# Attention and a squared-relu feed-forward on one core: down-stage blocks formed from consecutive 128-token tiles

## The chip, the cores and the metric

The kernel runs on one core of a Trainium2 chip. The metric is the device time of an execution in microseconds (us); the time before is the median of three runs. The engines are TensorE (PE; its weight loads are PEld), VectorE (DVE), ScalarE (ACT), GpSimd (POOL) and SyncE (SP, which here issues stores and transposing DMAs). Each engine runs its own instruction stream in order; semaphores tie them together.

## The reference

```
scores = 1/sqrt(64) * q @ k.T            # 8 batches, 16 query heads on 4 kv heads, 384 tokens, 64 wide
x      = softmax(scores) @ v             # put back as 3072 tokens x 1024
h      = max(x @ w_in, 0)                # w_in 1024 x 2048
out    = (h * h) @ w_out                 # w_out 2048 x 1024, out 3072 x 1024 float32
```

## The kernel before

**Stages.** A batch is 384 tokens, three tiles of 128. Attention works in 64 units p, eight per batch (two heads each): scores in two halves of three PSUM banks, an exponential on ACT over each half (L482), attention products into the bank `po` (L495), a reciprocal and a multiplication on DVE (L503, L505), and a transposing DMA into xT. The feed-forward of a batch has an up stage of 16 tiles (128 of the 2048 hidden columns by 384 tokens; eight chunks of contraction, L536): the tile is evicted by DVE with the relu into `hr` (L542) and squared by ACT into h2T (L550). In the last batch POOL squares the odd tiles (L547). The down stage multiplies h2T by w_out.

**Two down stages.** Batches 0 and 1 use plain products (row_down, L585). From batch 2 on the work is done in blocks with seven products instead of eight, in Strassen's manner: a block takes one 128-token tile of each of two batches as two row halves, halves of the 2048 hidden columns, and halves of the 1024 output columns. Sums of weights are formed once (w_sums). The sums of the left side are formed by DVE for each block (a_sums: sums 1, 2 and 4 go into the buffer a_late, sum 3 overwrites h2T). down_pair handles tile i of batch 2m with tile i of batch 2m+1, for i = 0, 1, 2, after the up stages of both. The products go in the order 1, 6, 7, 2, 5, 4, 3; the last, 3, of the last block of a pair is put off (`carry`) to behind the next up tile, and at the very end it is done in two parts of 384 and 128 columns (L675), each added and stored by itself.

**Two row halves.** Each matmul uses 64 of the array's 128 rows; the lower half (lo) and the upper half (hi) of one contraction are separate instructions that overlap. `push` writes out all lo pieces of a job (an up tile is 8 pieces of 162.5 ns, a product 8 pieces of 216 ns), and puts its hi pieces into the queue `behind`; they follow 450 ns or more later by a clock that the program keeps while it writes the instructions. What follows a job (eviction, square, sums) is put in when its last hi piece is out, through the list `late` where it is delayed. A job takes one of four PSUM banks and frees it after its hi pieces. The program's clock decides order only; on the chip semaphores decide.

**Handing out.** The main loop over n (unit n from 8 to 64) writes score half 0, fill(0.4), the attention products of unit n-1, score half 1, fill(0.6). `fill(share)` adds the share to a credit and takes items from the feed-forward generator as long as the credit is above zero; an item costs its ns divided by PACE for its kind (up or down) and batch. An item is a whole up tile, a chunk of a plain product group, or a whole product. A batch's up stage may start when its last transposed x is taken to have landed (`usable`); until then the generator gives nothing and the credit is set to 0.

**Order of batches.** Up 0, down 0, up 1, down 1, up 2, up 3, three blocks, up 4, up 5, three blocks, up 6, up 7, three blocks. Two tiles of the even batch's up stage are held back (HELD) and come behind the odd batch's sixteen, which run in the order c, c + 8. The first block's sums are formed in two halves, at once after the square of the tile that completes them (`half`, `then`).

Of the kernel before, what the change touches and what calls it, by code (L numbers as in the profile page):

```python
# [106 lines left out]
def bass_gqa_attention__then__ffn_squared_relu_kernel(  # L107
# [326 lines left out]
    def push(lo, hi, done=None, prev=None, frees=()):  # L434
        while prev is not None and not prev["over"]:
            clock["lo"] += 100.0
            catch_up(clock["lo"])
        after = [prev["last"]] if prev is not None else ()
        total = 0.0
        for ns, fn in lo:  # L440
            catch_up(clock["lo"])
            last = fn(after)
            after = ()
            clock["lo"] += ns
            total += ns
        job = dict(hi=list(hi), ready=clock["lo"] + GAP, after=[last], done=done, over=False, frees=frees)
        behind.append(job)
        return job, total
# [40 lines left out]
    def row_attend(p, then=None):  # L489
# [27 lines left out]
        last_av[0] = push(lo, hi, done, last_av[0])[0]  # L517
# [4 lines left out]
    last_up = [None]  # L522

# [5 lines left out]
    def row_up(b, c, r, then=None):  # L529
# [11 lines left out]
        def done():  # L541
            R.add("vector", lambda e: e.tensor_scalar_max(hr[r][:, :], acc[:, 0:S], 0.0),  # L542
                  reads=[key], writes=[("hr", r)])

            def square():
                if b == B - 1 and c % 2:
                    R.add("gpsimd", lambda e: e.tensor_tensor(h2T[b % 2][:, c, :], hr[r][:, :], hr[r][:, :], ALU.mult),  # L547
                          reads=[("hr", r)], writes=h2(b, c))
                else:
                    R.add("scalar", lambda e: e.activation(h2T[b % 2][:, c, :], hr[r][:, :], AF.Square),  # L550
                          reads=[("hr", r)], writes=h2(b, c))
                if then:
                    then()

            late.append((clock["hi"] + 750.0, square))

        lo, hi = ([piece(h, kc) for kc in range(NKC)] for h in range(2))
        job, total = push(lo, hi, done, frees=(i,))
        last_up[0] = job
        return "up", total  # L560
# [7 lines left out]
    def store(y, b, i, jj, c0=0, c1=512):  # L568
        rows = out[b * S:(b + 1) * S, :].rearrange("(p j) f -> j p f", j=NJ)[i]
        R.add("sync", lambda e: e.dma_start(rows[:, jj * 512 + c0:jj * 512 + c1], y_sb[y][:, c0:c1]),  # L570
              reads=[("y", y)], writes=[("out", b, i, jj, c0)], dma=f"y{y}_{c0}")

    def row_down(b, jj):
        banks, jobs = [None] * NJ, [None] * NJ
        chunks = ((0, 6), (6, 11), (11, 16))
        for c0, c1 in chunks:
            for i in range(NJ):
# [20 lines left out]
                jobs[i], total = push(lo, hi, done if end else None, jobs[i], (banks[i],) if end else ())  # L598
                yield "down", total
# [27 lines left out]
    def a_sums(i, slots, which, c0=0, c1=NHC):  # L627
        t = slice(i * 128, i * 128 + 128)
        s1, s2, s4 = slots
        cs, ds = slice(c0, c1), slice(NHC + c0, NHC + c1)  # L630
        A11, A12, A21, A22 = (h2T[x][:, y, t] for x in range(2) for y in (cs, ds))
        k11, k12, k21, k22 = ([("h2T", x, y + c, i) for c in range(c0, c1)] for x in range(2) for y in (0, NHC))
        k1, k2, k4 = ([("a_sum", x, c) for c in range(c0, c1)] for x in slots)
        if 1 in which:
            tensor_op(a_sum[s1][:, cs], A21, A22, ALU.add, k21 + k22, k1 + EARLY_A)
# [7 lines left out]
    def product(n, m, i, slots, bank, first, done, prev=None, frees=()):  # L643
        s1, s2, s4 = slots
        t = slice(i * 128, i * 128 + 128)
        left = {1: (h2T[0], 0, 0, t), 2: (h2T[0], NHC, 0, t), 4: (h2T[1], NHC, 1, t), 7: (h2T[1], 0, 1, t),
                3: (a_sum[s4], 0, s4, None), 5: (a_sum[s1], 0, s1, None), 6: (a_sum[s2], 0, s2, None)}[n]
# [3 lines left out]
        def operands_of(c):  # L651
            a, c0, x, tt = left
            lk = ("a_sum", x, c) if tt is None else ("h2T", x, c0 + c, i)
            rk = {1: ("w_out", 0), 2: ("w_out", 0), 3: ("w_out", 1)}.get(n, ("wt", {4: 4, 5: 1, 6: 2, 7: 3}.get(n), c // 2))
            return a[:, c0 + c, :] if tt is None else a[:, c0 + c, tt], lk, rk

        def piece(h, c):
            rows = ROWS[h]
            lhs, lk, rk = operands_of(c)
            return 216.0, lambda after: R.add(  # L660
                "tensor", lambda pe: pe.matmul(acc, lhs[rows], right[rows, c], start=(first and h == 0 and c == 0),  # L661
                                               stop=(h == 1 and c == NHC - 1), skip_group_check=True),
                reads=[lk, rk], writes=[key], after=after)

        if callable(done):
            lo, hi = ([piece(h, c) for c in range(NHC)] for h in range(2))
            return push(lo, hi, lambda: done(acc, key), prev, frees)
# [13 lines left out]
        return None, 1.0  # L681

    def down_pair(m, slots):

        b0, b1 = 2 * m, 2 * m + 1
        final = b1 == B - 1
# [4 lines left out]
        def p1(q):  # L691
# [6 lines left out]
            q["p1"], t = product(1, m, q["i"], (0, 0, 0), q["e"], True, done)  # L698
            return "down", t

        def rest(q):
            i = q["i"]
            sl = q["slots"] = slots[i]
            alone = final and i == NJ - 1

            def run(n, bank, first, done, prev=None, frees=()):
                job, t = product(n, m, i, sl, bank, first, done, prev, frees)
                return job, ("down", t)

            bank = next_bank()  # L710
            yield run(6, bank, True, lambda acc, key: add(q["u"], q["u"], acc, key), frees=(bank,))[1]
            bank = next_bank()
            q["v"] = next_y()
            yield run(7, bank, True, lambda acc, key: add(q["v"], q["u"], acc, key), frees=(bank,))[1]

            def c11(acc, key):
                y = next_y()
                R.add("scalar", lambda e: e.copy(y_sb[y][:, :], acc), reads=[key], writes=[("y", y)])
                store(y, b0, i, 0)
                if i + 1 < NJ:  # L720
                    slots[i + 1] = take_sums()
                    a_sums(i + 1, slots[i + 1], (1, 2, 3))

            yield run(2, q["e"], False, c11, q["p1"], (q["e"],))[1]
            q["g"] = next_bank()

            def c22(acc, key):
                y = next_y()
                add(y, q["v"], acc, key)
                store(y, b1, i, 1)  # L730
                if i + 1 < NJ:
                    a_sums(i + 1, slots[i + 1], (4,))
                if alone:
                    add(q["u"], q["u"], acc, key)

            q["p5"], t = run(5, q["g"], True, c22, frees=(q["g"],) if alone else ())
            yield t

            def c21(acc, key):
                y = q["v"]  # L740
                tensor_op(y_sb[y][:, :], y_sb[y][:, :], acc, ALU.subtract, [key, ("y", y)], [("y", y)])
                store(y, b1, i, 0)

            bank = next_bank()
            yield run(4, bank, True, c21, frees=(bank,))[1]

        def p3(q):
            i = q["i"]

            def c12(acc, key):  # L750
                add(q["u"], q["u"], acc, key)
                store(q["u"], b0, i, 1)

            if final and i == NJ - 1:
                def part(f0, f1):
                    def fn(acc, key):
                        u = q["u"]
                        tensor_op(y_sb[u][:, f0:f1], acc[:, f0:f1], y_sb[u][:, f0:f1], ALU.add, [key, ("y", u)], [("y", u)])
                        store(u, b0, i, 1, f0, f1)
                    return f0, f1, fn  # L760

                return "down", product(3, m, i, q["slots"], None, True, [part(0, 384), part(384, 512)])[1]
            return "down", product(3, m, i, q["slots"], q["g"], False, c12, q["p5"], (q["g"],))[1]

        q = dict(i=0)
        yield p1(q)
        until(last_up[0])
        settle()
        upped.update((b0, b1))
        for i in range(NJ):  # L770
            yield from rest(q)
            if i + 1 < NJ:
                after = dict(i=i + 1)
                yield p1(after)
                yield p3(q)
                q = after
        carry.append(lambda: p3(q))

    HELD = 2
    tiles = [0]  # L780
    by_rows = [False]
    carry = []
    w_todo = [(n, part) for part in range(4) for n in (3, 2, 4)] + [(1, part) for part in range(4)]
# [20 lines left out]
    def feed_forward(b):  # L804
# [6 lines left out]
        order = [(b, c) for c in range(first, NFC)]  # L811
        if paired:
            order = [(b, c) for g in range(NHC) for c in (g, g + NHC)] + [(b - 1, c) for c in range(NFC - HELD, NFC)] \
                if b % 2 else order[:-HELD]
        slots = {}

        def half(x, which):
            if 0 not in slots:
                slots[0] = take_sums()
            a_sums(0, slots[0], which, x * NHC // 2, (x + 1) * NHC // 2)  # L820

        then = {}
        if paired and b % 2:
            then = {NHC - 1: lambda: half(0, (1, 2, 3, 4)), NFC - 1: lambda: half(1, (1, 2, 3)), len(order) - 1: lambda: half(1, (4,))}
        for n, (bb, c) in enumerate(order):
            if by_rows[0]:
                yield row_up(bb, c, tiles[0] % NHR, then.get(n))
            else:
                for k in range(0, NKC, 4):
                    yield up_step(bb, c, k, k + 4, tiles[0] % 2, tiles[0] % NHR)  # L830
            tiles[0] += 1
            if carry:
                yield carry.pop()()
# [4 lines left out]
        if paired and b % 2:  # L838
            yield from down_pair(b // 2, slots)
        elif not paired:  # L840
            last = last_up[0]
            for jj in range(2):
                for kind in row_down(b, jj):
                    yield kind
                    if last and last["over"]:
                        upped.add(b)


    def all_feed_forward():
        for b in range(B):  # L850
            while usable.get(b, float("inf")) > clock["lo"]:
                if carry:
                    yield carry.pop()()
                yield None
            yield from feed_forward(b)
        while carry:
            yield carry.pop()()
# [3 lines left out]
    PACE = {1: (3200.0, 3200.0), 2: (3700.0, 3100.0), 3: (3700.0, 3100.0), **{b: (5800.0, 3800.0) for b in range(4, B + 1)}}  # L861
# [124 lines left out]
```

The softmax here doesn't subtract the row's maximum and nothing guards it: scores larger than these inputs give would overflow.

## Time and profile before

| | us |
|---|---|
| median of three runs | 425.43 (425.27 to 425.53) |
| profiled execution, its own time | 424.85 |
| its span, first to last instruction | 422.8 |
| ACT exponential, one (L482, 112 of them) | 1.131 |
| ACT square, one (L550, 114) | 0.519 |
| POOL square, one (L547, 8) | 0.827 |
| DVE relu eviction, one (L542, 122) | 0.557 |
| DVE addition of a product to y, one (L603) | 0.69 |
| store of a y tile, issue to landing (L570, 47) | 2.0 |

Times in windows and timelines count from the first instruction. A window's row gives, for each engine, busy us and the number of instructions in brackets, in the order PE, PEld, DVE, ACT, POOL, then the granted clock (1.00 is full), the DMA share and GB/s. In the list of waits the numbers are us in total, times, and the longest in us. In a timeline a row is start, duration, engine, line, operation, out<-in, and in square brackets the idle time before it and what ended it. A matmul's end in these records is modelled, so two matmuls that follow each other overlap in them.

### The profile page before, as it was taken

The page shows a single profiled execution, that of the slowest core. Times are in us where ns is not written, and L with a number is a line of the kernel's source. Part 1 is how long each engine was busy: PE and PEld are TensorE (multiplying, and loading weights), DVE is VectorE, ACT ScalarE, POOL GpSimd, SP SyncE. Part 2 cuts the span into 40 slices and gives each one's busy share as a digit, 9 for nine tenths or more (in the row PEclk, how much of TensorE's full clock was granted, in tenths as well). Part 3 has the DMA queues.
Part 4 walks back from the last instruction along what each step waited for, and adds up shares of the span by engine and source line. Part 5 has one row for each costly group of instructions (what it writes and reads, how often), then busy time and mean ns, then how long its engine had stood idle before and what let it go on. Part 6 is the DMA issues. An engine that isn't in the chain of part 4 may idle for free.

```text
span 422.8 us, 13245 instructions
## 1 busy us (share of the span) xinstructions
PE 409.2 (97%) x6061; PEld 311.7 (74%) x6061; DVE 202.5 (48%) x419; ACT 213.0 (50%) x276; POOL 55.1 (13%) x70
## 2 busy tenths in 40 slices
PE   7999999999999999999999999999999999999995
PEld 4666877678767777877767788887676788858883
DVE  2664424278332555464563354555554354455442
ACT  4855764367755566665544556666554423112100
POOL 5831001021003000300021001200000000320000
PEclk9999999999999999999999999999999999999998
DMA  8999999639729931971229910980213220000222
GB/s 229 197 197 202 206 191 165 152 75 131 130 62 120 201 82 22 118 121 27 96 76 198 220 44 14 128 128 20 95 47 120 70 71 2 2 2 24 76 101 99
DMA packets 96103, 45.02 MB, mean 106 GB/s; under 512 B 74416, under 2 KB 90032, under 8 KB 96048
## 3 DMA queue, kind: packets, MB, share of 16 engines
q0 software_dynamic: 34288, 16.65, 31.6%
q1 hardware_dynamic: 58720, 25.28, 27.4%
q10 hardware_dynamic: 3040, 2.26, 1.8%
q8 instruction: 47, 0.77, 0.8%
q14 instruction: 8, 0.07, 0.0%
HBM read 35.65 MB, written 12.58 MB: 114 GB/s over the span
## 4 chain that ended last, share of the span: by engine, by line
PE 89%; ACT 4%; DVE 4%; DMA 2%; issue 1%; ACTq 0%; POOL 0%; DVEq 0%
PE sc_ps L536 16%; PE f_ps L536 16%; PE sc_ps L661 12%; PE f_ps L661 12%; PE po L495 12%; PE sc_ps L478 8%; PE f_ps L585 5%; ACT expT L482 3%; PE sc_ps L585 3%; PE f_ps L791 2%; DMA w_late<-in_q_dram 1%; DVE o_sb L505 1%; PE po L378 1%; PE sc_ps L361 1%; PE sc_ps L300 1%
## 5 line engine op out<-in xcount | busy, mean ns | idle before, releaser
L482 ACT ACTIVATE expT<-sc_ps 128x1152 bf16<-128x1152 f32 x112 | 126.7, 1131 | 102.1 <-PE sc_ps L478 64.1
L536 PE MATMUL sc_ps<-xT,w_in_sb 64*128 64x384 bf16 x992 | 146.6, 322 | 0.7 <-DVE hr L542 0.7
L536 PE MATMUL f_ps<-xT,w_in_sb 64*128 64x384 bf16 x960 | 142.2, 323 | 0.0
L536 PEld LDWEIGHTS sc_ps<-xT,w_in_sb 64*128 64x128 f16 x992 | 83.4, 94 | 15.3 <-DVE hr L542 1.1
L536 PEld LDWEIGHTS f_ps<-xT,w_in_sb 64*128 64x128 f16 x960 | 80.9, 94 | 13.2
L495 PEld LDWEIGHTS po<-v_aug,expT 64*128 64x128 bf16 x2016 | 76.1, 94 | 18.3 <-DVE o_sb L505 9.6
L550 ACT ACTIVATE h2T<-hr 128x384 bf16<-128x384 f32 x114 | 58.3, 519 | 52.6 <-DVE hr L542 52.6
L495 PE MATMUL po<-v_aug,expT 64*128 64x65 bf16 x2016 | 81.6, 190 | 2.3 <-DVE o_sb L505 2.1
L478 PE MATMUL sc_ps<-qT,kT 64*128 64x384 bf16 x336 | 57.1, 323 | 3.3 <-ACT expT L482 2.6
L542 DVE TENSOR_SCALAR hr<-f_ps 128x384 f32<-128x384 f32 x60 | 33.4, 557 | 38.9 <-PE f_ps L536 24.3
L542 DVE TENSOR_SCALAR hr<-sc_ps 128x384 f32<-128x384 f32 x62 | 34.3, 556 | 36.0 <-PE sc_ps L536 20.0
L661 PE MATMUL sc_ps<-w_out_sb,a_late 64*128 64x512 f16 x176 | 42.1, 376 | 0.0
L585 PE MATMUL sc_ps<-w_out_sb,h2T 64*128 64x512 f16 x192 | 41.5, 376 | 0.0
L585 PE MATMUL f_ps<-w_out_sb,h2T 64*128 64x512 f16 x192 | 39.7, 376 | 0.0
L661 PE MATMUL f_ps<-w_out_sb,h2T 64*128 64x512 f16 x160 | 38.7, 376 | 0.0
L661 PE MATMUL f_ps<-w_late,h2T 64*128 64x512 f16 x160 | 38.5, 376 | 0.0
L503 DVE RECIPROCAL rinv<-po 128x6 f32<-128x6 f32 x56 | 10.9, 195 | 47.5 <-PE sc_ps L585 16.8
L478 PEld LDWEIGHTS sc_ps<-qT,kT 64*128 64x128 bf16 x336 | 23.5, 94 | 13.6 <-ACT expT L482 9.9
L505 DVE TENSOR_TENSOR o_sb<-po,rinv 128x384 bf16<-128x384 f32 x56 | 31.2, 557 | 2.1 <-DVE rinv L503 0.2
L661 PE MATMUL sc_ps<-w_late,h2T 64*128 64x512 f16 x128 | 31.2, 376 | 0.0
L661 PE MATMUL sc_ps<-w_out_sb,h2T 64*128 64x512 f16 x128 | 30.9, 376 | 0.0
L603 DVE TENSOR_TENSOR y_sb<-sc_ps,y_sb 128x512 f32<-128x512 f32 x20 | 13.7, 691 | 26.3 <-PE sc_ps L661 15.0
(102 smaller groups left out, 426.4 us busy)
## 6 DMA issues: line engine op xcount, KB each, us to landing
out_dram<-y_sb SPq DMA_DIRECT2D x47, 256.0 KB, 2.0
q_next<-in_q_dram POOLq DMA_DIRECT2D x7, 768.0 KB, 10.6
w_in_sb<-in_moe_w_in_dram POOLq DMA_DIRECT2D x8, 512.0 KB, 12.4
w_out_sb<-in_moe_w_out_dram POOLq DMA_DIRECT2D x2, 2048.0 KB, 33.3
k_st<-in_k_dram POOLq DMA_DIRECT2D x7, 192.0 KB, 4.2
v_st<-in_v_dram POOLq DMA_DIRECT2D x7, 192.0 KB, 11.5
xT<-o_sb SPq DMA_TRANSPOSE x56, 3.0
w_late<-in_q_dram ACTq DMA_DIRECT2D x1, 768.0 KB, 8.6
```

Source lines behind the costliest of these rows:

```text
L478: "tensor", lambda pe: pe.matmul(sc_ps[:, i, 0:S], kt[rows, j * 128:(j + 1) * 128], qt[rows, :]),
L482: R.add("scalar", lambda e: e.activation(expT[p % NEX][:, 3 * half:3 * half + 3, :], sc_ps[:, 0:3, 0:S], AF.Exp, scale=0.125), reads=[("sc ...
L495: "tensor", lambda pe: pe.matmul(po_v[:, f % NJ, f // NJ, :], expT[p % NEX][rows, 2 * j + f % 2, f // 2 * 128:f // 2 * 128 + 128], v_aug[b ...
L503: R.add("vector", lambda e: e.reciprocal(rinv_v, po_v[:, :, :, D:D + 1]), reads=["po"], writes=[("rinv", p % 2)])
L505: R.add("vector", lambda e: e.tensor_tensor(o_sb[p % NO][:, :, :, :], po_v[:, :, :, 0:D], rinv_v.to_broadcast([128, NJ, 2, D]), ALU.mult), ...
L536: "tensor", lambda pe: pe.matmul(acc[:, 0:S], w_in_sb[rows, kc, c * 128:(c + 1) * 128], xT[b % NXT][rows, kc, :], start=(h == 0 and kc == ...
L542: R.add("vector", lambda e: e.tensor_scalar_max(hr[r][:, :], acc[:, 0:S], 0.0), reads=[key], writes=[("hr", r)])
L550: R.add("scalar", lambda e: e.activation(h2T[b % 2][:, c, :], hr[r][:, :], AF.Square), reads=[("hr", r)], writes=h2(b, c))
L585: "tensor", lambda pe: pe.matmul(acc, h2T[b % 2][rows, c, i * 128:(i + 1) * 128], w_out_sb[rows, c, jj * 512:(jj + 1) * 512], start=(h == ...
L603: R.add("vector", lambda e: e.tensor_tensor(out_ap, a, b, op), reads=reads, writes=writes)
L661: "tensor", lambda pe: pe.matmul(acc, lhs[rows], right[rows, c], start=(first and h == 0 and c == 0), stop=(h == 1 and c == NHC - 1), skip ...
L791: m = pe.matmul(acc[:, 0:S], w_in_sb[:, kc, c * 128:(c + 1) * 128], xT[b % NXT][:, kc, :], start=(kc == 0), stop=(kc == NKC - 1))
```

## The change

Blocks are formed from consecutive 128-token tiles: the tiles of batch 2, 3, 4 ... are put in a row, and after each up stage as many pairs as are complete are done: one block after batches 2, 4 and 6, two after 3, 5 and 7. The order becomes up 2, one block, up 3, two blocks, up 4, one block, and so on. A left-over tile (the third of an even batch) is paired with the first of the next batch. No tiles are held back; every batch from 2 on runs its up tiles in the order c, c + 8. The first block's sums are formed in three pieces (chunks 0-3, 4-6, 7), each written out 1.5 us, by the program's clock, after the square that completes it. All squares of up tiles are on ACT. `squared` records which squares have been written out; a product whose left side is read straight from h2T waits in the program's clock for it.

push becomes push_steps, a generator that gives control back whenever 800 ns or more of lo work have been written and more is left, so that an item of `fill` is a part of a tile or product. The hi pieces still go to `behind` when the whole lo half is written. PACE for batch 2 goes from (3700, 3100) to (4300, 3400), for batch 3 from (3700, 3100) to (5200, 3500). In the last product's two parts, the addition writes and the store reads a key of its own for each part.

```diff
+    STEP = 800.0
+    def push_steps(lo, hi, done=None, prev=None, frees=()):
...
-        for ns, fn in lo:
+        for n, (ns, fn) in enumerate(lo):
             catch_up(clock["lo"])
             last = fn(after)
             after = ()
             clock["lo"] += ns
             total += ns
+            if total >= STEP and n + 1 < len(lo):
+                yield total
+                total = 0.0
...
+    def staged(kind, steps):
+        while True:
+            try:
+                ns = next(steps)
+            except StopIteration as stop:
+                return stop.value
+            yield kind, ns
...
             def square():
-                if b == B - 1 and c % 2:
-                    R.add("gpsimd", lambda e: e.tensor_tensor(h2T[b % 2][:, c, :], hr[r][:, :], hr[r][:, :], ALU.mult),
...
+                squared.add((b, c))
                 if then:
-                    then()
+                    late.append((clock["hi"] + 1500.0, then))
...
-    def store(y, b, i, jj, c0=0, c1=512):
+    def store(y, b, i, jj, c0=0, c1=512, key=None):
...
-              reads=[("y", y)], writes=[("out", b, i, jj, c0)], dma=f"y{y}_{c0}")
+              reads=[key or ("y", y)], writes=[("out", b, i, jj, c0)], dma=f"y{y}_{c0}")
...
+            def emit(after):
+                if not isinstance(left, int):
+                    while (left[0], left[1] + c) not in squared:
+                        clock["lo"] += 100.0
+                        catch_up(clock["lo"])
...
-                        tensor_op(y_sb[u][:, f0:f1], acc[:, f0:f1], y_sb[u][:, f0:f1], ALU.add, [key, ("y", u)], [("y", u)])
-                        store(u, b0, i, 1, f0, f1)
+                        tensor_op(y_sb[u][:, f0:f1], acc[:, f0:f1], y_sb[u][:, f0:f1], ALU.add, [key, ("y", u)],
+                                  [("y", u, f0)])
+                        store(u, x0, i0, 1, f0, f1, ("y", u, f0))
...
+        q = block(0)
+        yield from p1(q)
         until(last_up[0])
         settle()
-        upped.update((b0, b1))
-        for i in range(NJ):
+        for n in range(len(pairs)):
             yield from rest(q)
...
-            order = [(b, c) for g in range(NHC) for c in (g, g + NHC)] + [(b - 1, c) for c in range(NFC - HELD, NFC)] \
-                if b % 2 else order[:-HELD]
...
+            order = [c for g in range(NHC) for c in (g, g + NHC)]
+            rows.extend((b, i) for i in range(NJ))
+            while len(rows) > 1:
+                pairs.append((rows.pop(0), rows.pop(0)))
+            slots[0] = take_sums()
+            for c0, c1 in ((0, 4), (4, NHC - 1), (NHC - 1, NHC)):
+                then[2 * c1 - 1] = lambda c0=c0, c1=c1: a_sums(pairs[0], slots[0], (1, 2, 3, 4), c0, c1)
...
-    PACE = {1: (3200.0, 3200.0), 2: (3700.0, 3100.0), 3: (3700.0, 3100.0), **{b: (5800.0, 3800.0) for b in range(4, B + 1)}}
+    PACE = {1: (3200.0, 3200.0), 2: (4300.0, 3400.0), 3: (5200.0, 3500.0), **{b: (5800.0, 3800.0) for b in range(4, B + 1)}}
```

## The prediction, made before the changed kernel was run

> **What bounds the kernel now.** I read the page first, then the windows by stage, the waits, and the timeline around single stalls.
>
> ```profile
> span 422.8 us, 13245 instructions
> ...
> PE 409.2 (97%) x6061; PEld 311.7 (74%) x6061; DVE 202.5 (48%) x419; ACT 213.0 (50%) x276; POOL 55.1 (13%) x70
> ...
> PE 89%; ACT 4%; DVE 4%; DMA 2%; issue 1%; ACTq 0%; POOL 0%; DVEq 0%
> ```
>
> TensorE carries the chain; the rest is waiting. From here on "U" is a batch's up stage (16 tiles), "P" one block of seven products. The windows, stage by stage (U1 and the direct down stages until 150; U2, U3; three P; U4, U5; three P; U6, U7; the end):
>
> ```profile
> 40.00:80.00 40.00, 39.13 (x646) 31.15 (x641) 13.67 (x29) 20.95 (x26) 2.30 (x2) 1.00 1.23 192
> 80.00:150.00 70.00, 68.09 (x1150) 51.77 (x1146) 35.19 (x70) 43.47 (x51) 10.00 (x10) 1.00 0.81 120
> 150.00:190.00 40.00, 39.98 (x666) 32.08 (x668) 21.96 (x45) 24.92 (x37) 4.95 (x5) 1.00 0.53 78
> 190.00:240.00 50.00, 48.85 (x774) 35.45 (x771) 24.09 (x48) 26.10 (x28) 4.95 (x5) 1.00 0.62 113
> 240.00:290.00 50.00, 50.00 (x826) 42.82 (x822) 25.69 (x54) 30.92 (x45) 4.96 (x5) 1.00 0.56 87
> 290.00:340.00 50.00, 48.90 (x772) 34.70 (x768) 23.99 (x47) 25.85 (x28) 0.00 (x0) 1.00 0.24 78
> 366.00:381.00 15.00, 14.30 (x175) 9.67 (x172) 7.10 (x16) 2.55 (x5) 4.96 (x6) 1.00 0.01 2
> ```
>
> PE is full in the up stages and loses time in the down stages and before 150. The page understates it: a matmul's modelled end (0.32 or 0.38 us) reaches past its slot (0.163 us for 384 columns, 0.216 for 512, on each of two row halves). Measured from start to start, the array idles 12.0 us after 36 us in stalls over 0.15 us: 6.3 before scores (L478), 4.5 before attention products (L495), 0.9 before an up tile (L536), 0.2 at the last product. The waits name the releasers:
>
> ```profile
> PEld sc_ps L478 <- ACT expT L482: 9.9, 23, 0.9
> PEld po L495 <- DVE o_sb L505: 9.6, 19, 0.9
> DVE y_sb L603 <- DMA out_dram<-y_sb: 1.9, 1, 1.9
> ```
>
> A typical one, PE then ACT:
>
> ```profile
> 328.38 0.49 PE L478 MATMUL sc_ps<-qT,kT 64*128 64x384 bf16 x3
> 329.15 0.28 PE L495 MATMUL po<-v_aug,expT 64*128 64x65 bf16 x4
> 330.12 0.49 PE L478 MATMUL sc_ps<-qT,kT 64*128 64x384 bf16 x3 [0.61 <-ACT expT L482]
> 328.93 1.13 ACT L482 ACTIVATE expT<-sc_ps 128x1152 bf16<-128x1152 f32 x1 [2.43 <-PE sc_ps L478]
> ```
>
> Both score halves use banks 0 to 2, so the second waits for the first's exponential. Here only attention's own products stood between them; no feed-forward work was handed out, and 0.82 us is lost.
>
> **What the Trainium skill says.** "Perfetto Trace Analysis", Identifying the Most-Contended Engine: matmul busy time doesn't measure closeness to the peak; agreed, 97% hides the 12 us. "TensorE: Matmul & The Clock Gate", The mechanism: matmuls start in program order; agreed, at 330.12 what was ready behind the scores stayed behind them. The same page, Architectural detail, calls ACT's and DVE's queues strict FIFOs; agreed below at 368. "DMA: Bandwidth & Descriptors", Anatomy of one DMA, gives a fixed cost of about 2.0 us on GpSimd's path; the SP stores here show 1.6 to 2.0.
>
> **The change, part by part.** Products stay 9 blocks of 7, up tiles 128, so PE's work is unchanged (about 389 us of array time).
>
> *Zero hand-outs.* fill(share) adds to a credit and hands out items while it is above 0, each costing ns/pace. Before, a product costs 1728/3800 = 0.455; the credit can sink to -0.455, and fill(0.4) then gives nothing. Worked from n = 8 (10 tiles of U0 left, credit 0), this happens at n = 26, 38, 43, 57, 62, and the trace has just these stalls: 126.4 (0.57 and 0.28 us), 195 (0.16, 0.70), 221.5 (0.85), 303.5 (0.26, 0.59), 330.1 (0.82), together 4.2 us. After, a step is at most 864 ns (four pieces of 216; an up tile 812 + 488): cost 0.227 at most at this pace. Credit stays above -0.227, so every fill(0.4) gives a step: 864 at least, on both halves once hi work is queued; the worst of these stalls lost 0.85, so it just fills them. Gain 4.2 (3.4 if each keeps 0.15).
>
> *Short hand-outs before scores.* Where the 0.6 fill gave 1300 or 1296, scores waited 0.25 to 0.31 (n = 9, 11, 17, 22, 29, 30); where both of n = 16 gave 1080, 0.36 and 0.39: 2.4 us, a threshold near 1.55. New credits, with PACE 4300/3400 and 5200/3500 for batches 2 and 3: 1788 and 2112 in batch 1; left are n = 16 (1080, 0.36), 22 and 26 (1296, 0.25 each), 24 (1512, 0.05), 0.9. Gain 1.5. The first stall (0.74 at 38.4, a square ahead of the exponential) stays.
>
> *Attention products waiting for po.* 3.5 us remain beside the zero cases. Two hand-outs that sum to 2600 give 0.41 to 0.64; sums from 3088 none before the P stages; nine sums of 3456 in P stages 0.54 in all, 0.06 each. After: n = 10 to 15 have 3084 to 3456 (none); n = 16 has 3024 for 2592 (0.61 becomes 0.2); n = 23 2592 (0.47), 25 2808 (0.25); ten of 3456 at 0.06. Sum 1.5; gain 2.0.
>
> *Squares on ACT, the delayed block sums, no held tiles.* In the last batch POOL squared odd tiles, and the sums went into DVE's queue at once:
>
> ```profile
> 368.82 0.83 POOL L547 TENSOR_TENSOR h2T<-hr 128x384 bf16<-128x384 f32 x1 [0.47 <-DVE hr L542]
> 369.68 0.43 DVE L603 TENSOR_TENSOR a_late<-h2T 128x512 bf16<-128x512 bf16 x1 [0.94 <-POOL h2T L547]
> 371.16 1.01 DVE L542 TENSOR_SCALAR hr<-sc_ps 128x384 f32<-128x384 f32 x2
> ```
>
> DVE waited 0.94 for POOL and did four sums (1.6 us); the evictions behind came late and PE lost 0.91 at 371.8. After: ACT's 0.52 replaces POOL's 0.83 (eight squares, 4.2 us, on an ACT 17% busy there), and the sums come 1.5 us later. Gain 0.9. DVE gets more sums, 84 for 48: a 512-wide one is 0.42, a 1024-wide 0.68, hence 0.36 and 0.22 (estimates by the line through these) for 384 and 128; 6 x 4 x (0.42+0.36+0.22) + 3 x 4 x 0.68 = 32 us for 26. At 48% busy this hides; only an eviction caught behind a burst would show, below.
>
> *The tail.* Both parts of the last tile had one key, so the second addition waited for the first part's store:
>
> ```profile
> 418.01 0.56 DVE L603 TENSOR_TENSOR y_sb<-f_ps,y_sb 128x384 f32<-128x384 f32 x1 [0.72 <-PE f_ps L675]
> 420.51 0.29 DVE L603 TENSOR_TENSOR y_sb<-f_ps,y_sb 128x128 f32<-128x128 f32 x1 [1.95 <-DMA out_dram<-y_sb]
> ```
>
> With a key per part it starts at 418.57. The second store is issued 0.35 after its end as now, and ends near 420.9, with the first landing at about 420.5. Gain 1.9 (1.6 if the stores slow each other).
>
> *What is added: six changes from up to down instead of three, without the two held tiles.* Call T the end of the last tile's lo half. Its hi half ends at T + 1.75 (450 ns gap, 1300 of work); eviction 0.56, square 0.52, two small sums 0.44, four hand-overs of 0.1 (0.06 from the end of the scores at 328.87 to the exponential at 328.93, rounded up): T + 3.7. Product 6 needs the last chunk at T + 1.73 + 1.51 = T + 3.2. So 0.4 is late where nothing lies between; a score block between hides it, but its exponential can put 1.13 ahead of the square. For even batches product 1 reads tile 14 of the same batch (ready about T + 1.75, wanted at T + 1.51): 0.2. Behind the waiting matmul stands all of PE, scores too. Bounds per change 0 to 1.7; I take 0.35, in all 2.1. The planner's own waits (until the last up job is over; `squared`) are lo time without work: three more of 0.1 to 0.3, and split jobs leave small misfits: 0.7 (0 to 1.5).
>
> *Order of batches.* U3, U5, U7 start one P later, and the new pace leaves 57.6 us of feed-forward after the last attention instead of 70.1 (credits). x is in time: U2 from n = 27 needs attention to n = 24, U3 n = 34 against 32, U5 51 against 48; U1 starts 4104 + 1080 + 1296 ns of items and two score blocks of 0.49 after its last attention, 7.5 us; needed are that unit's own hi half (2.2 of queue, 0.6) and the 3.5 that the code allows for landing (the page: 3.0), 6.3. No cost; if one came late, about 1 us. POOL's and SP's loads move with n only.
>
> Sum: 4.2 + 1.5 + 2.0 + 0.9 + 1.9 = 10.5 off, 2.8 on: 7.7 off. The profiled execution took 424.85 (span 422.8 and 2.05 around it), hence 417.15; the median of the runs is 0.6 higher, 425.43, so **417.7 us**.
>
> **Rivals.**
> 1. *Only the certain parts:* zero hand-outs, tail and POOL give 7.0; the finer cutting brings nothing at scores and po, and the changes cost 3.5: 425.4 - 3.5 = 421.9. For it: small sums leave little margin at 864. Against: the threshold of 1.55 fitted nine stalls. 0.22.
> 2. *Slower: the square chain uncovered.* If at each change an exponential stands before the last square and DVE before the eviction, the last sum arrives at T + 3.7 + 1.13 + 0.7 = T + 5.5 against T + 3.2, and product 1 waits too: some 2.5 each, 15 in all; 425.4 - 10.5 + 15 = 430. It decides from 1.75 per change on. For it: the held tiles that covered it go; against: an exponential in front mostly means scores and attention products (1.1 us of PE work) in front as well. 0.07.
> 3. *Nearly all stalls go:* changes free, added misfits none: 425.4 - 11.5 = 414. Up stages with attention already show PE full. 0.10.
> 4. *The stalls only move* to the new changes and the time is the same: 425. 0.04.
>
> **How the numbers follow.** Main case 0.57, its own range 414.5 to 420.5 (change cost 0 to 5, misfits 0 to 1.5). 0.2%, about 0.85 us, is what a measurement can tell. Faster: main, 1 and 3, 0.89; same 0.04; slower 0.07. The range 412.5 to 423 leaves out rivals 2 and 4 and a little of the tails.
>
> **What would show it.** Right: no pair of score halves with attention products alone between them; L478's wait for expT near 3 us instead of 9.9; no DVE wait for the out store; no POOL L547 group; DVE never waiting 0.9 before block sums. Wrong: PE waiting before L661-type products for a_late or h2T at six places by over a microsecond; PE waiting for xT; scores stalling after 864 ns steps; two stores at the end taking over 2.5 us.

## The result, and the profile after

The changed kernel takes 419.24 us (median of four runs, 419.18 to 420.13) against 425.35: a ratio of 0.9861, with a 95% interval of 0.9844 to 0.9878, so it is faster by 1.4%. Its profiled execution took 419.18, with a span of 417.2.

The page, then four of the windows cut as before, then the waits:

```profile
span 417.2 us, 13267 instructions
PE 407.6 (98%) x6061; PEld 308.1 (74%) x6061; DVE 207.1 (50%) x455; ACT 216.7 (52%) x284; POOL 48.5 (12%) x62
```

```profile
40.00:80.00 40.00, 39.86 (x661) 32.31 (x660) 14.02 (x30) 22.45 (x26) 2.30 (x2) 1.00 1.25 193
80.00:150.00 70.00, 69.98 (x1169) 57.12 (x1167) 38.93 (x75) 41.49 (x52) 10.05 (x10) 1.00 0.78 122
150.00:190.00 40.00, 39.04 (x646) 31.34 (x643) 20.27 (x46) 22.86 (x32) 4.12 (x4) 1.00 0.56 76
240.00:290.00 50.00, 48.85 (x797) 40.69 (x793) 25.21 (x57) 28.88 (x40) 4.96 (x5) 1.00 0.72 101
```

```profile
PEld sc_ps L500 <- ACT expT L504: 3.2, 7, 0.9
PEld po L517 <- DVE o_sb L527: 1.9, 7, 0.3
PEld f_ps L689 <- DVE a_late L621: 3.1, 4, 1.4
PEld sc_ps L689 <- ACT h2T L569: 2.0, 2, 1.5
```

(L500, L517, L559 and L689 are L478, L495, L536 and L661 of before.) Until 150 us PE is nearly full now. The wait for the exponential fell from 9.9 to 3.2 and that for po from 9.6 to 1.9; new are waits of products for the block sums (`a_late`) and for h2T. Two of the windows shown lose about 1 us; each has a change from up to down in it, at 163 and at 257.

Counted from matmul start to matmul start as in the prediction, with stalls over 0.15 us named (at the changes of the changed kernel, two of 0.12 and 0.15 as well):

| lost array time, us | before | after |
|---|---|---|
| scores waiting for an exponential | 6.3 | 1.6 |
| attention products waiting for po | 4.5 | 0 |
| up tile behind the sums that waited for POOL | 0.9 | 0 |
| the six changes from up to down | (0.16, counted at po) | 5.9 |
| last product | 0.2 | 0.2 |
| smaller gaps | 2.8 | 3.4 |

That is 3.7 us less (the rows, rounded, give 3.6); with 1.9 less at the end it is the difference of the spans, 5.6.

The six places, in order of time, lose 1.15, 0.35, 1.36, 1.04, 0.97 and 0.98. Here is the last one, where no attention runs beside it: DVE, ACT (the line with h2T<-hr), and PE.

```profile
388.52 0.35 DVE L621 TENSOR_TENSOR a_late<-h2T 128x384 bf16<-128x384 bf16 x1
...
389.44 0.35 DVE L621 TENSOR_TENSOR a_late<-h2T,a_late 128x384 bf16<-128x384 bf16 x1
389.71 0.55 DVE L565 TENSOR_SCALAR hr<-f_ps 128x384 f32<-128x384 f32 x1
390.30 0.52 ACT L569 ACTIVATE h2T<-hr 128x384 bf16<-128x384 f32 x1 [1.14 <-DVE hr L565]
390.85 0.23 DVE L621 TENSOR_TENSOR a_late<-h2T 128x128 bf16<-128x128 bf16 x1 [0.59 <-ACT h2T L569]
391.40 0.39 PE L689 MATMUL sc_ps<-w_late,a_late 64*128 64x512 f16 x1 [0.59 <-DVE a_late L621]
```

Evictions came every 1.30 us, the one before at 388.04, so the last was due at 389.34; four sums of chunks 4 to 6 (two of them shown) stood ahead of it and held it to 389.71. Then eviction, square and two small sums run one after the other with nothing left to give PE. In the third change the square itself is late, behind an exponential:

```profile
257.14 1.13 ACT L504 ACTIVATE expT<-sc_ps 128x1152 bf16<-128x1152 f32 x1 [1.16 <-PE sc_ps L500]
258.17 0.51 ACT L569 ACTIVATE h2T<-hr 128x384 bf16<-128x384 f32 x1
258.74 0.39 PE L689 MATMUL sc_ps<-w_out_sb,h2T 64*128 64x512 f16 x1 [1.15 <-ACT h2T L569]
```

The end is as the key makes it: the second addition follows the first at once.

```profile
414.18 0.56 DVE L621 TENSOR_TENSOR y_sb<-sc_ps,y_sb 128x384 f32<-128x384 f32 x1 [0.72 <-PE sc_ps L705]
414.65 0.28 DVE L621 TENSOR_TENSOR y_sb<-f_ps,y_sb 128x128 f32<-128x128 f32 x1
```

### The profile page after: what moved, and what is told of

It is laid out like the page before. It is cut to its first block, busy times and chain, and to the rows that moved or that the text cites. A ratio compares the mean times of both kernels' runs of the same rounds, so it can differ in the third digit from the quotient of the medians.

```text
span 417.2 us, 13267 instructions
## 1 busy us (share of the span) xinstructions
PE 407.6 (98%) x6061; PEld 308.1 (74%) x6061; DVE 207.1 (50%) x455; ACT 216.7 (52%) x284; POOL 48.5 (12%) x62
## 4 chain that ended last, share of the span: by engine, by line
PE 91%; DVE 4%; ACT 2%; DMA 1%; issue 1%; ACTq 0%; POOL 0%; DVEq 0%
PE sc_ps L559 18%; PE f_ps L559 17%; PE sc_ps L689 12%; PE po L517 12%; PE f_ps L689 11%; PE sc_ps L500 7%; PE sc_ps L603 5%; PE f_ps L603 4%; PE f_ps L824 2%; DMA w_late<-in_q_dram 1%; DVE a_late L621 1%; PE po L378 1%; ACT expT L504 1%; DVE hr L565 1%; PE sc_ps L361 1%; ACT h2T L569 1%
## 5 line engine op out<-in xcount | busy, mean ns | idle before, releaser
L559 PE MATMUL sc_ps<-xT,w_in_sb 64*128 64x384 bf16 x976 | 152.0, 322 | 0.0
L559 PE MATMUL f_ps<-xT,w_in_sb 64*128 64x384 bf16 x976 | 148.4, 322 | 0.0
L559 PEld LDWEIGHTS sc_ps<-xT,w_in_sb 64*128 64x128 f16 x976 | 83.7, 94 | 13.0
L559 PEld LDWEIGHTS f_ps<-xT,w_in_sb 64*128 64x128 f16 x976 | 84.2, 94 | 10.9
L569 ACT ACTIVATE h2T<-hr 128x384 bf16<-128x384 f32 x122 | 62.2, 519 | 48.7 <-DVE hr L565 48.0
L517 PEld LDWEIGHTS po<-v_aug,expT 64*128 64x128 bf16 x2016 | 77.4, 94 | 11.5 <-DVE o_sb L527 1.9
L517 PE MATMUL po<-v_aug,expT 64*128 64x65 bf16 x2016 | 81.4, 190 | 0.0
L500 PE MATMUL sc_ps<-qT,kT 64*128 64x384 bf16 x336 | 57.8, 323 | 0.7 <-ACT expT L504 0.5
L689 PE MATMUL sc_ps<-w_out_sb,a_late 64*128 64x512 f16 x192 | 47.1, 376 | 0.0
L603 PE MATMUL sc_ps<-w_out_sb,h2T 64*128 64x512 f16 x192 | 41.6, 376 | 0.0
L603 PE MATMUL f_ps<-w_out_sb,h2T 64*128 64x512 f16 x192 | 40.6, 376 | 0.0
L689 PE MATMUL f_ps<-w_out_sb,h2T 64*128 64x512 f16 x160 | 39.4, 376 | 0.0
L689 PE MATMUL f_ps<-w_late,h2T 64*128 64x512 f16 x160 | 39.0, 376 | 0.0
L689 PE MATMUL sc_ps<-w_out_sb,h2T 64*128 64x512 f16 x128 | 32.0, 376 | 1.3 <-ACT h2T L569 1.1
L689 PE MATMUL sc_ps<-w_late,h2T 64*128 64x512 f16 x128 | 31.4, 376 | 0.0
L500 PEld LDWEIGHTS sc_ps<-qT,kT 64*128 64x128 bf16 x336 | 25.1, 94 | 6.7 <-ACT expT L504 3.2
L621 DVE TENSOR_TENSOR y_sb<-sc_ps,y_sb 128x512 f32<-128x512 f32 (+1 forms) x21 | 14.4, 685 | 24.7 <-PE sc_ps L689 15.9
```

Source lines behind the costliest of these rows:

```text
L500: "tensor", lambda pe: pe.matmul(sc_ps[:, i, 0:S], kt[rows, j * 128:(j + 1) * 128], qt[rows, :]),
L517: "tensor", lambda pe: pe.matmul(po_v[:, f % NJ, f // NJ, :], expT[p % NEX][rows, 2 * j + f % 2, f // 2 * 128:f // 2 * 128 + 128], v_aug[b ...
L559: "tensor", lambda pe: pe.matmul(acc[:, 0:S], w_in_sb[rows, kc, c * 128:(c + 1) * 128], xT[b % NXT][rows, kc, :], start=(h == 0 and kc == ...
L603: "tensor", lambda pe: pe.matmul(acc, h2T[b % 2][rows, c, i * 128:(i + 1) * 128], w_out_sb[rows, c, jj * 512:(jj + 1) * 512], start=(h == ...
L621: R.add("vector", lambda e: e.tensor_tensor(out_ap, a, b, op), reads=reads, writes=writes)
```

## The experiments

Each ratio is against the kernel before, run beside it on the same chip; the changed kernel stands at 0.9861. The question was where the 5.6 us of span came from: from the finer steps, the pairing or the pace.

**The key alone** (the kernel before with the store's key).

> The kernel before with nothing but a key of its own for each part of the last tile. Theory A: the second addition starts at once, 1.9 us less, 423.4. Rival: the two stores then run together and slow each other, or something else ends last, under 1 us less, 424.5 or more.

Measured 423.35, ratio 0.9952 (0.9936 to 0.9968): 2.0 us, as theory A has it. The tail is settled, and the two stores cost each other nothing that shows.

**Whole items again, all else as changed.**

```diff
-    STEP = 800.0
+    STEP = 1e9
```

> The changed kernel with whole items handed out again (STEP so large that push_steps never gives back inside a job); pairing, pace, key and squares stay as changed. Theory A (the finer steps remove the waits for the exponential and for po; the new pairing only costs): worked through the credits, fill(0.4) gives nothing at n = 43 and 57 (0.85 each), 0.6 fills of 1300 or less return at nine places (0.25 to 0.45) and five attention products come after 2160 to 2600 (about 0.5): some 6.5 us come back, 425.5. Theory B (the stalls went because down stages stand in turn with up stages and the pace is slower, the steps matter little): within 1.5 us of the changed kernel, 418 to 421.

Measured 427.91, ratio 1.0063 (1.0040 to 1.0086): slower than before, and 2.4 us slower than even theory A expected. The trace has the waits for exponentials and po back, up to 0.90 (at 117.5), and still loses time at the six changes. Pairing and pace without the finer steps are a loss, 2.6 us even with the tail's 2.0 us of gain in it.

**The finer steps alone**, on the kernel before (with the changed kernel's waits for `squared` in the program's clock).

> The kernel before (pairing after two up stages, two tiles held, its pace, POOL squares, sums at once, one key) with the finer hand-out alone. Theory A: the credits leave no empty fill; of the 6.3 us before scores 1.4 stay, of the 4.5 us before attention products 0.2; 9.3 us less, 416: below the changed kernel. Theory B: at most 2 us less, 423 or more.

Measured 425.55, ratio 1.0007 (0.9997 to 1.0017): nothing won, against theory A. But the stalls went as theory A says: over 0.15 us there are four before scores, 1.7 in all, and none of the old ones before po. In their place stands a single stall. SP, then DVE, then PE:

```profile
219.91 5.18 SPq L331 DMA_TRANSPOSE kT<-k_dup  x1
227.66 5.03 SPq L338 DMA_TRANSPOSE qT<-q_next  x2
232.73 0.58 SPq L592 DMA_DIRECT2D out_dram<-y_sb  x1
235.30 0.69 DVE L625 TENSOR_TENSOR y_sb<-f_ps,y_sb 128x512 f32<-128x512 f32 x1 [10.68 <-DMA out_dram<-y_sb]
236.13 0.56 DVE L527 TENSOR_TENSOR o_sb<-po,rinv 128x384 bf16<-128x384 f32 x1
236.74 0.23 PE L517 MATMUL po<-v_aug,expT 64*128 64x65 bf16 x1 [7.08 <-DVE o_sb L527]
```

SP issued k's transpose at 219.91, 6 us after the loads of k, q and v (before: 9 us). q landed only at 227.6, and SP waited 2.6 us for it; the transposes of k and q held SP for another 10.2 us. A store of y stood behind them all and went out at 232.73. The addition that needed that y buffer waited 10.7 us on DVE, the reading of po stood behind it, and PE lost 7.3 us. The Trainium skill, "DMA: Bandwidth & Descriptors", Anatomy of one DMA, says that the wait for a semaphore happens on the issuing engine before dispatch; the 2.6 us are such a wait. The reading at this point was that attention had got faster, and that the stores of three blocks in a row therefore met the next batch's transposes; the runs that follow try it.

**The old pairing with everything else but the pace**, and **the same with earlier loads**. The second has one more edit:

```diff
-            row_attend(n - 1, load_next if c == 1 and 2 <= b < B - 1 else None)
+            row_attend(n - 1, load_next if c == (1 if b == 2 else 0) and 2 <= b < B - 1 else None)
```

> The changed kernel with the old pairing (three blocks after two up stages, two tiles held) and the old pace; the finer steps, the key, ACT squares and the delayed sums stay. In the run with the finer steps alone one stall of 7.3 us at 236.7 took back the gain: SP stood at the transposes of q, whose load had not landed, a store of y stood behind them, DVE's addition waited for that store, and the reading of po stood behind it. Theory C (that stall belongs to the old pairing's three blocks in a row, which fall on the load and the transposes of the next batch): it stays, 7 us and a slower clock after it, less 1.9 for the key and 0.9 for POOL: 422.5. Theory D (a chance meeting that any shift of the order undoes): it goes, 414.

> The same with one more edit: the loads of the next batch's k, q and v are issued one unit n earlier from batch 3 on (about 4.3 us). Theory C: q has landed when SP reaches its transposes, the store is no longer held, the 7.3 us stall goes, 413.5 to 414.5, below the changed kernel. Rival: what holds the store is the slow issue of the transposes themselves (5.2 us for k), and the stall only shrinks: 418 or more.

The first: 422.34, ratio 0.9919 (0.9892 to 0.9946), as theory C has it; the stall is there with 6.1 us (235.8). The second: 417.87, ratio 0.9802 (0.9753 to 0.9850), executions from 415.3 to 419.4. In its profiled execution, one of 415.27, the stall shrank to 2.1 (231.2), with DVE still 5.5 on the store. That lies between the two expectations: the stall only shrinks, as the rival says, and the time is a little under the rival's 418. SP in that execution:

```profile
219.55 1.99 SPq L331 DMA_TRANSPOSE kT<-k_dup  x1
221.59 3.35 SPq L338 DMA_TRANSPOSE qT<-q_next  x2
```

The wait for q, 2.0 us in the first of the two runs, is gone, and the transposes of k and q themselves take 5.3 us instead of 9.4. So the store went out 5.4 us after the start of k's transpose instead of 11.4; it then took 4.7 us to land instead of 2.6. The load of q that came too late for SP is the smaller part of what was won; the slow transposes are the larger. The two executions near 419 had a mean granted clock of 0.996, the two faster ones 1.000, which fits a longer stall in the slow ones (the last section has stalls and clock); that the spread of 4 us comes from there is likely, but not shown. This version, with none of the new pairing, is not slower than the changed kernel.

**The old pace on the changed kernel.**

```diff
-    PACE = {1: (3200.0, 3200.0), 2: (4300.0, 3400.0), 3: (5200.0, 3500.0), **{b: (5800.0, 3800.0) for b in range(4, B + 1)}}
+    PACE = {1: (3200.0, 3200.0), 2: (3700.0, 3100.0), 3: (3700.0, 3100.0), **{b: (5800.0, 3800.0) for b in range(4, B + 1)}}
```

> The changed kernel with the old pace for batches 2 and 3, nothing else. By the credits only n = 16 has short hand-outs then; three short ones (0.6 us) go. If the pairing alone removes the meeting of stores and transposes: 418.5 to 419.5, no change. If the slower pace is what removes it: a stall of several us comes back, 422 or more.

Measured 426.74, ratio 1.0016 (0.9997 to 1.0035). The same meeting comes back, this time through ACT:

```profile
237.99 0.58 ACT L745 COPY y_sb<-f_ps 128x512 f32<-128x512 f32 x1 [6.13 <-DMA out_dram<-y_sb]
238.47 1.14 ACT L504 ACTIVATE expT<-sc_ps 128x1152 bf16<-128x1152 f32 x1
```

A copy to y waited 6.1 us for a store, the exponential stood behind it, and the scores lost 4.6 us (at 239.7). That is 4.6 of the 7.4 us by which the span is longer than the changed kernel's; the 3.4 us at half clock after it cost an estimated 1.7 more. So the pairing alone doesn't avoid the meeting, and three blocks in a row aren't needed for it, since here there are two. With this pairing the new pace, which hands out more feed-forward work per unit of attention, does avoid it, but not by making the transposes quick. In the changed kernel they hold SP for 10 us as well:

```profile
230.10 4.60 SPq L331 DMA_TRANSPOSE kT<-k_dup  x1
235.03 5.13 SPq L338 DMA_TRANSPOSE qT<-q_next  x2
```

The stores before them went out by 229.7, and nothing waits for the next one, at 240.2.

**The new pace with the old pairing**, without and with the earlier loads.

> The changed kernel with the old pairing and the two held tiles, but with the new pace for batches 2 and 3; finer steps, key, ACT squares and delayed sums stay. Theory E (the new pace keeps the stores clear of the transposes, the pairing only adds the six changes at 5.9 us): no long stall, 413 to 414, some 5.5 below the changed kernel. Theory C (three blocks in a row meet the transposes whatever the pace): a stall of 4 to 7 us and 419 or more.

> The old pairing with the new pace and with the loads of k, q, v one unit earlier from batch 3 on. If what is left of SP's hold-ups in that version is the load of q: 0.5 to 1.5 below it and less spread between executions. If none is left: the same within 0.3.

Measured 436.83, ratio 1.0252 (1.0231 to 1.0274), and 435.46, 1.0222 (1.0201 to 1.0244). Theories E and C both missed this. The window from 150 to 182, of the first of the two and of the changed kernel:

```profile
150.00:182.00 32.00, 23.37 (x338) 17.39 (x335) 8.52 (x20) 16.29 (x19) 4.12 (x4) 0.68 0.33 46
```

```profile
150.00:182.00 32.00, 31.04 (x518) 24.36 (x515) 16.66 (x39) 18.18 (x24) 4.12 (x4) 1.00 0.30 56
```

More feed-forward work per unit of attention uses up what there is: without a block between U2 and U3, U3 is due before the x of batch 3, the generator gives nothing, and attention stands alone: no matmul of an up tile starts from 160 to 178.5, and each unit stalls once before its attention products (1.1 us) and once before scores (1.7 us). In the changed kernel the block after U2 (about 159 to 174) fills just this place. Besides these there is one stall of 1.5 us at 240.5, scores behind an exponential that stood behind a copy to y. The earlier loads gave 1.4 us, which was within the expectation, but the spread stayed at 2 us and the intervals of the two overlap.

Pairing and pace now stand crossed, all else as changed (ratios to the kernel before):

| | old pace | new pace |
|---|---|---|
| old pairing, two tiles held | 0.9919 | 1.0252 |
| new pairing | 1.0016 | 0.9861 |

From 0.9919, each of the two is a loss without the other; together they gain.

**The block sums split otherwise** on the changed kernel: after tile 13 sums 1 and 2 alone.

```diff
-            for c0, c1 in ((0, 4), (4, NHC - 1), (NHC - 1, NHC)):
-                then[2 * c1 - 1] = lambda c0=c0, c1=c1: a_sums(pairs[0], slots[0], (1, 2, 3, 4), c0, c1)
+            then[7] = lambda: a_sums(pairs[0], slots[0], (1, 2, 3, 4), 0, 4)
+            then[13] = lambda: a_sums(pairs[0], slots[0], (1, 2), 4, NHC - 1)
+
+            def rest_of_sums():
+                a_sums(pairs[0], slots[0], (1, 2), NHC - 1, NHC)
+                a_sums(pairs[0], slots[0], (3, 4), 4, NHC)
+
+            then[15] = rest_of_sums
```

> The changed kernel with the block sums split another way: after tile 13 only sums 1 and 2 of chunks 4 to 6 (0.7 instead of 1.5 us on DVE), sums 3 and 4 of chunks 4 to 7 after the last square. Theory A1 (at each of the six changes from up to down the four sums stand on DVE ahead of the last tile's eviction and hold it up 0.4 to 0.9): the 5.9 us lost at the changes fall by about 2.5, 416.7. Theory A2 (the exponential ahead of the last square on ACT sets the end, except in the last two changes, which have hardly any attention beside them): 0.8 less, 418.4.

Measured 419.23, ratio 0.9853 (0.9837 to 0.9870): no difference from the changed kernel, so both expectations missed, A2 by less. The last change went from 0.98 to 0.48 and the second from 0.35 to 0, the first to about 0.8, but the third and fourth, with an exponential before the square, kept 1.36 and 1.07, and two new waits for po (0.38 each) stand behind the sums that were moved. The sums ahead of the eviction explain a part only.

**Cover at the changes:** product 4 of the last block before an up stage is put off to just before the next block's product 1. Three versions were run, with product 3 behind the first, second or third tile of the next up stage:

```diff
-            bank = next_bank()
-            yield from run(4, bank, True, c21, frees=(bank,))
+            def p4():
+                bank = next_bank()
+                yield from run(4, bank, True, c21, frees=(bank,))
+
+            if hold and n + 1 == len(pairs):
+                put_off.append(p4)
+            else:
+                yield from p4()
...
         q = block(0)
+        if put_off:
+            yield from put_off.pop()()
         yield from p1(q)
...
-            if carry:
+            if carry and n:
                 yield from carry.pop()()
```

The last two changed lines belong to the second version; the third has `n > 1`, the first leaves `if carry:` as it was.

> The changed kernel with product 4 of the last block before an up stage put off to just before the next block's product 1, so that at five of the six changes 1.73 us of product work stand between the last up tile and the first product that needs its squares. Theory A (the lost time at the changes is the bare latency of eviction, square and sums, 5.9 us in six places): five of them fall under 0.2, 4.7 us less, 414.5. Rival (the wait moves with the product, since the exponential and the sums shift too): under 2 us less, 417.5 or more.

Measured 423.44, ratio 0.9940 (0.9915 to 0.9964): both expectations missed. Five of the six changes are clean, only the first, which has nothing put off, keeps 1.15; but five new stalls of 1.05 stand where product 3 follows:

```profile
174.70 0.39 PE L689 MATMUL sc_ps<-w_out_sb,a_late 64*128 64x512 f16 x1 [0.79 <-DVE y_sb L621]
```

Products 5 and 3 share a bank, and DVE's addition of 5 must read it before 3 adds to it; product 4 had stood between. The stalls alone don't make the run 4 us slower than the changed kernel. Ahead of the one shown a single row half runs for some 0.8 us, since what comes next on the other waits already (172.9 to 173.7); counted as array time over 9 us around each, the five places lose 1.4 to 2.0 us, 8.8 in all, against 4.7 won at the changes.

> The kernel with product 4 put off, with the block's product 3 one up tile later (behind the second tile of the next up stage instead of the first). In the run before, product 3 came so soon after product 5 that it waited 1.05 us for DVE to read their common bank, at five places. Expected: these 5.3 us go and the changes stay covered, 414 to 418; if a third bank held through two up tiles stalls the up tiles instead, 421 or more.

Measured 416.93, ratio 0.9791 (0.9773 to 0.9810), within the expected range; four waits of 0.50 to 0.68 are left there.

> Product 4 put off as before, product 3 behind the third tile of the next up stage. In the run before, product 3 still waited 0.50 to 0.68 us at four places for DVE's addition out of the bank it shares with product 5. Expected: these 2.2 us go, 414.7; the first change, which has no put-off product, keeps its 1.15. If three banks are too few for three up tiles, a wait of an up tile for an eviction appears at each of those places and the time stays at 416.5 to 417.5.

Measured 414.97, ratio 0.9747 (0.9723 to 0.9770), against an expectation of 414.7. All are gone; of stalls over 0.19 us the trace has the first change (1.16), four score waits (1.6) and the last product. This version is faster than both kernels: 10.8 us below the kernel before (425.73 beside it), where the change itself gave 6.1.

## Why the prediction was right, and which terms were mis-sized

Forecast were 417.7 in a range of 412.5 to 423, faster; it is 419.24. The mechanism of the gains was right. That the total came within 1.5 us is partly luck: the gains were taken 1.5 us too small and the costs 3.7 us too small, which partly cancels, and the new pace, priced at nothing, turned out to keep a stall of 4.6 us away. Point by point:

- *Zero hand-outs (4.2) and short hand-outs before scores (1.5):* right. The five stalls are gone; beside the first one at 38.3, which was forecast to stay, the stalls left are at 78.2, 111.8 and 130.2 with 0.37, 0.26 and 0.23, where the credits put n = 16, 22 and 26 (forecast 0.36, 0.25, 0.25). The run with whole items shows that it is the steps that do it.
- *po (2.0):* too small; all 3.5 went. The threshold taken from whole items didn't hold for divided ones: sums of 2592 and 2808 ns stalled no more. Why was not tried.
- *POOL and the delayed sums (0.9), tail (1.9):* right; the tail by itself measured 2.0. The stall of 0.9 is still there in the run with the finer steps alone and gone with ACT squares and delayed sums; which of the two removes it wasn't separated.
- *Six changes (2.1, at 0.35 each):* the term that failed, 5.9 and 0.98 each. The chain from eviction over square to sums was the right one; the cost was taken with the engines free. On DVE the four sums after tile 13 (1.2 us) stand ahead of the last eviction, which the prediction saw only as "an eviction caught behind a burst", and on ACT an exponential of 1.13 stands ahead of the square in the third and fourth, which it named and gave no share in the 0.35. Where neither stands ahead, the estimate holds: the last change, with its sums moved, kept 0.48. The put-off product shows the whole term: cover removes it at five places. Of the prediction's signs of being wrong, this one came in part: three of the six places lose over a microsecond.
- *Misfits (0.7):* 0.6 more in small gaps.
- *Order of batches and pace ("No cost"):* true of the changed kernel, but it was the wrong question. The prediction counted finer steps as a gain by themselves. They aren't: alone they won nothing, with the old pace the changed kernel loses everything, the tail's 2.0 included, and with the old pairing the new pace starves. The three parts carry each other, though earlier loads did as much for the old pairing and pace. In the trace of before no engine waits for a store there, but SP is held in the same place, by the transposes of k and q from 228.8 to 236.1; that was the sign to read.
- *Rivals:* rival 2 (slower) asked for 1.75 per change; 0.98 stayed below that. What it feared, an exponential ahead of the square, came at the third and fourth change, with 1.36 and 1.04 instead of some 2.5. The sum of gains, 12.0 instead of 10.5, and of costs, 6.5 instead of 2.8, gives 5.5, which is the 5.6 of the spans.

## What to carry to other kernels

Removing stalls speeds up the work that issues loads and stores, so look at what stands one after the other in the DMA-issuing queue, at how long each entry holds it, and whether the gap between a load and the instruction that waits for it shrinks. Where a chain over three engines must end before the next product, count what stands in each queue ahead of its links, and put a product there that depends on none of them. Check what that product stood between, since its place may have been cover as well.

## What the runs showed of the hardware that was not expected

A single stall of PE can cost more than its length. In the run with the finer steps alone, the stall of 7.3 us ended at 236.7, and the granted clock stood at half from 232.1 to 242.4:

```profile
232.10:242.40 10.30, 5.66 (x58) 4.07 (x60) 2.57 (x5) 1.13 (x1) 0.00 (x0) 0.50 0.51 146
```

Until then the matmuls of an up tile started every 0.32 us on a row half instead of every 0.16, so the stall cost an estimated 2.8 us more (half of the 5.7 us left). After the stall of 6.1 us the half clock lasted until 239.3, after that of 4.6 us from 240.0 to 243.4, and in the starved stage, whose stalls are of 1.1 to 1.7 us each, it held from 161.4 to 185.3. The stall of 2.1 us and the single stalls of up to 1.4 us in the changed kernel left the clock at 1.00. The Trainium skill, "TensorE: Matmul & The Clock Gate", What's actually happening, has the clock follow how busy PE was of late, and these traces agree.

A transposing DMA holds SP longer while loads are under way. Over all traces here, one of k held SP for 1.5 to 2.0 us in the 15 cases where no load of k, q or v was in flight, and for 1.5 to 5.8 us, with a median of 3.2, in the 69 where one was.
